# Splitting score chunks 9 to 7 and 10 to 6 between TensorE and VectorE at the layer ends of a two-layer decode kernel, with the last softmax moved ahead of V work

## Chip, cores, metric

One core of a Trainium2 chip. The metric is the device time of one execution in microseconds (us), lower is better. The runs of one kernel spread over 0.5 to 1.5 us here, and the differences of this case are of the same order, so medians and ranges are given.

## The reference, cut

Batch 2, one token, width 576, two identical layers. Each has an attention block over a given cache of 16384 keys and values (32 heads, head size 128, bfloat16) and an MLP block (576 to 4608 to 576).

```python
def _A_ref(x, k_cache, v_cache, wq, wo):
    q = (x @ wq).reshape(B, 1, 32, 128).transpose(0, 2, 1, 3)
    scores = jnp.einsum("bhqd,bhkd->bhqk", q, k_cache) * 128 ** -0.5
    p = softmax(scores)
    o = jnp.einsum("bhqk,bhkd->bhqd", p, v_cache)
    return o.transpose(0, 2, 1, 3).reshape(B, 1, 4096) @ wo
# _B_ref: layernorm, a shift term with w2, layernorm, gelu(. @ w3) @ w4, residuals
x = x + A(layernorm(x));  x = x + B(layernorm(x))     # layer 0
x = x + A(layernorm(x));  x = x + B(layernorm(x))     # layer 1, same weights and cache
```

The K and V loads are 126 x 8.39 MB = 1.06 GB for two layers, with almost no reuse: this is a stream from HBM.

## The kernel before

There are 64 *units* per layer (2 batches x 32 heads). A unit is one K and one V of 4 MiB. Its 128 blocks of 128 keys are cut into 16 *chunks* of 8. VectorE and TensorE share the score work:

- a chunk on TensorE is 8 transposes into PSUM, an eviction by ScalarE, and 8 one-column matmuls (the lines with `tps`, `ktsb`, `sps`);
- a chunk on VectorE (a *dot*) is one multiply by the broadcast query and one reduction (`prod`, `sd`).

V work (a *weighing*, `ops`) is 128 one-column matmuls. SBUF holds three *places*, each one K and one V; the weights reuse the same space, so loads wait until the tenant before is done. One queue (SyncE's) issues all loads in a fixed order. Layer 1 runs the units backwards, so the last two units of layer 0 stay in SBUF.

```python
W4_PIECES = (6, 3, 2, 1)          # w4 in 12 parts; the first piece shares w3's place
...
self.NCP = self.NCH // 2          # 8 of 16 chunks on TensorE, always
...
def weigh(self, l, i, h):
    vt, res = self.get("V", l, u, h)      # res: the loads of this half (two for the split last unit)
    def f(pe):
        for j in range(self.TB):
            ins = pe.matmul(self.ops[q][:, 0:1], lhsT=vt[:, j * 128:(j + 1) * 128], rhs=..., ...)
        return ins
    self.pe(f, r=[*res, f"p{q}"], w=[f"P:ops{q}"])
    self.release("V", l, u, h)
...
def attention(self, l):           # one unit per turn of the loop
    for i in range(U):
        early = l == 1 and 1 <= i <= 4
        dv = list(range(NCP, NCH))
        for c in range(NCP):
            self.turn(l, i, c)                       # transposes and eviction
            if len(self.waiting) > self.LEAD: self.score()
            if i >= 1 and c == 1: self.unit_max(l, i - 1)
            if i >= 1 and c == (3 if early else 4): self.exps(l, i - 1)
            if c >= 1:
                for _ in range(-(-len(dv) // (NCP - c))): self.dots(l, i, dv.pop(0))
            if i == U - 1 and c == 3:                # the "mid projection"
                self.weigh(l, i - 2, 0); self.weigh(l, i - 2, 1)
                self.normalize(*mid, ...); self.project_pieces(l, [self.n_wo - 1])
        now = i >= 1 and not early and i != U - 2
        if now: self.weigh(l, i - 1, 0)
        while self.waiting: self.score()
        if now: self.weigh(l, i - 1, 1)
        self.row_max(l, i)
        ...
    self.unit_max(l, U - 1); self.exps(l, U - 1); self.normalizers(...)
    self.normalize(other, ...)
    self.weigh(l, U - 1, 0); self.weigh(l, U - 1, 1)
    ...                                              # last projection, then the MLP
```

The mid projection matters for loads: the last quarter of the last V lies where wo's last piece lies, so it can't be loaded before. In layer 0 only one place is free for weights (the other two hold the kept units), so w4's later pieces wait until the first row blocks of w3 are used, and layer 1's wq waits for w3 and for w4's first piece.

Of the kernel before, what the change touches and what calls it, by code (L numbers as in the profile page):

```python
# [233 lines left out]
class Decode:  # L234
# [5 lines left out]
    ROT = 12  # L240
    WO_PIECE = 4
    FJ = 3
    W4_PIECES = (6, 3, 2, 1)

    def __init__(self, nc, A_x, K, V, wq, wo, w2, w3, w4, out):
        self.nc = nc
        self.A_x, self.K, self.V, self.wq, self.wo = A_x, K, V, wq, wo
        self.w2, self.w3, self.w4, self.out = w2, w3, w4, out
        self.B, Sq, self.D = A_x.shape
        _, self.H, self.S, self.Dh = K.shape  # L250
        self.F = w3.shape[1]
        assert Sq == 1 and self.Dh == 128 and self.B == 2
        self.KT = (self.D + 127) // 128
        self.klast = self.D - 128 * (self.KT - 1)
        self.p0 = 128 - self.klast
        assert self.p0 == 64
        self.MT = self.F // 128
        self.FA = self.MT // self.FJ
        assert sum(self.W4_PIECES) == self.FA
        self.U = self.B * self.H  # L260
        self.NB = self.S // 128
        self.TB = self.NB // 2
        self.NCH = self.NB // self.CH
        self.NCP = self.NCH // 2
        self.scale = float(self.Dh) ** -0.5
        n = self.H - 1 - self.N_MID
        self.n_wo = -(-n // self.WO_PIECE) + 1
        cuts = [*range(0, n, self.WO_PIECE), n, self.H - 1]
        self.wo_cuts = [cuts, [self.H - c for c in cuts]]
        self.s = Sched(nc)  # L270
        sb = nc.alloc_sbuf_tensor
        B, KT = self.B, self.KT
        self.half = self.TB * 128
        self.place_n = 4 * self.half
        self.buf = sb("buf", [128, 3 * self.place_n], BF16)
        self.ring = Arena(self.s, self.buf)
        self.ktsb = [sb(f"ktsb{i}", [128, self.CH, 128], BF16) for i in range(self.NKT)]
        self.prod = [sb(f"prod{i}", [128, self.CH, 128], BF16) for i in range(2)]
        self.ident = sb("ident", [128, 128], BF16)
        self.identS = sb("identS", [128, 128], FP32)  # L280
        self.qt = sb("qt", [128, self.U], BF16)
        self.qb = [sb(f"qb{i}", [128, 128], BF16) for i in range(2)]
        self.p = [sb(f"p{i}", [128, self.NB], BF16) for i in range(2)]
        self.sd = [sb(f"sd{i}", [128, self.TB], FP32) for i in range(2)]
        small = sb("small", [128, 11 + 4 * B], FP32)
        self.cinv, self.cone, self.ceps = small[:, 0:1], small[:, 1:2], small[:, 2:3]
        self.m1, self.m2, self.m, self.bias = (small[:, 3 + 2 * i:5 + 2 * i] for i in range(4))
        self.st = small[:, 11:11 + 2 * B].rearrange("p (a b) -> p a b", a=2)
        self.var, self.rstd = small[:, 11 + 2 * B:11 + 3 * B], small[:, 11 + 3 * B:11 + 4 * B]
        self.qcur = sb("qcur", [128, 2], BF16)  # L290
        self.wolast = sb("wolast", [128, self.D], BF16)
        self.lsum = sb("lsum", [128, self.U, 2], FP32)
        self.o = sb("o", [128, self.U], FP32)
        self.den = sb("den", [128, self.U], FP32)
        self.otn = sb("otn", [128, self.U], BF16)
        self.xa = sb("xa", [128, 2, KT, B], FP32)
        self.xb = sb("xb", [128, 2, KT, B], FP32)
        self.x1 = sb("x1", [128, 2, KT, B], FP32)
        self.hs = sb("hs", [128, KT, B], FP32)
        self.xc = sb("xc", [128, KT, B], FP32)  # L300
        self.xn = sb("xn", [128, KT, B], BF16)
        self.xnh = sb("xnh", [128, 2, B], BF16)
        self.sel = sb("sel", [128, 128], BF16)
        self.par = sb("par", [128, 2], FP32)
        self.xsum = sb("xsum", [128, KT, B], FP32)
        self.zero = sb("zero", [128, B], BF16)
        MB = self.MT * B
        flat = self.prod[0][:, :, :].rearrange("p a b -> p (a b)")
        self.zz, self.zu, self.ze, self.zr = (flat.bitcast(FP32)[:, i * MB:(i + 1) * MB] for i in range(4))
        self.gt = flat[:, 8 * MB:9 * MB]  # L310
        self.rows = flat[:, 0:self.D]
        ps = nc.alloc_psum_tensor
        self.tps = [ps(f"tps{i}", [128, self.CH * 128], BF16) for i in range(3)]
        self.sps = [ps(f"sps{i}", [128, 512], FP32) for i in range(2)]
        self.ops = [ps(f"ops{i}", [128, 512], FP32) for i in range(2)]
        self.misc = ps("misc", [128, 512], FP32)
# [348 lines left out]
    def query_rows(self, l, i):  # L665
# [4 lines left out]
        self.act(lambda a: a.activation(out=self.qb[q][:, :], in_=self.misc[:, 0:128], func=ACT.Copy),  # L670
                 r=["P:misc"], w=[f"qb{q}"])

    def turn(self, l, i, c):

        u = self.order[l][i]
        h, j0 = divmod(c * self.CH, self.TB)
        kt, res = self.get("K", l, u, h)
        b, k = c % 3, c % self.NKT

        def f(pe):  # L680
            for j in range(self.CH):
                ins = pe.transpose(self.tps[b][:, j * 128:(j + 1) * 128],  # L682
                                   kt[:, (j0 + j) * 128:(j0 + j + 1) * 128], self.ident[:, :])
            return ins
        self.pe(f, r=[*res, "ident"], w=[f"P:tps{b}"])
        self.act(lambda a: a.activation(out=self.ktsb[k][:, :, :].rearrange("p a b -> p (a b)"), in_=self.tps[b][:, :],  # L686
                                        func=ACT.Copy), r=[f"P:tps{b}"], w=[f"ktsb{k}"])
        self.waiting.append((l, i, c, k))
        if (c + 1) * self.CH == self.TB:
            self.release("K", l, u, 0)  # L690
# [13 lines left out]
    def dots(self, l, i, c):  # L704
        u = self.order[l][i]
# [4 lines left out]
        k3 = kt.rearrange("p (j d) -> p j d", d=128)[:, j0:j0 + self.CH, :]  # L710
        self.dve(lambda v: v.tensor_tensor(out=self.prod[d][:, :, :], in0=k3, in1=bcast_mid(self.qb[q][:, :], self.CH),  # L711
                                           op=ALU.mult), r=[*res, f"qb{q}"], w=[f"prod{d}"])
        o = c * self.CH - self.NCP * self.CH
        self.dve(lambda v: v.tensor_reduce(out=self.sd[q][:, o:o + self.CH], in_=self.prod[d][:, :, :], axis=AX.X,  # L714
                                           op=ALU.add), r=[f"prod{d}"], w=[f"sd{q}"])
        if (c + 1) * self.CH == self.NB:
            self.release("K", l, u, 1)

    def row_max(self, l, i):
        q = i % 2  # L720
        n = self.NCP * self.CH
        self.dve(lambda v: v.tensor_reduce(out=self.m1[:, q:q + 1], in_=self.sps[q][:, 0:n], axis=AX.X, op=ALU.max),  # L722
                 r=[f"P:sps{q}"], w=[f"m1{q}"])
        self.dve(lambda v: v.tensor_reduce(out=self.m2[:, q:q + 1], in_=self.sd[q][:, 0:self.NB - n], axis=AX.X,  # L724
# [12 lines left out]
    def exps(self, l, i):  # L737
        u = self.order[l][i]
        q = i % 2
        n = self.NCP * self.CH  # L740
        for part, (c0, c1, src, res) in enumerate(((0, n, self.sps[q][:, 0:n], f"P:sps{q}"),
                                                   (n, self.NB, self.sd[q][:, 0:self.NB - n], f"sd{q}"))):
            self.act(lambda a, c0=c0, c1=c1, src=src, part=part: a.activation(  # L743
# [4 lines left out]
    def weigh(self, l, i, h):  # L748
        u = self.order[l][i]
        q = i % 2  # L750
        vt, res = self.get("V", l, u, h)

        def f(pe):
            for j in range(self.TB):
                ins = pe.matmul(self.ops[q][:, 0:1], lhsT=vt[:, j * 128:(j + 1) * 128],  # L755
                                rhs=self.p[q][:, h * self.TB + j:h * self.TB + j + 1],
                                start=(h == 0 and j == 0), stop=(h == 1 and j == self.TB - 1))
            return ins
        self.pe(f, r=[*res, f"p{q}"], w=[f"P:ops{q}"])
        self.release("V", l, u, h)  # L760
        if h == 1 and i < self.U - 1:
            self.dve(lambda v: v.tensor_copy(out=self.o[:, u:u + 1], in_=self.ops[q][:, 0:1]),
                     r=[f"P:ops{q}"], w=["o"])
# [46 lines left out]
        self.project(parts[0][0], parts[-1][0] + parts[-1][1], parts)  # L810

    def attention(self, l):
        U, NCP, NCH = self.U, self.NCP, self.NCH
        self.waiting = []
        self.query(l, 0)
        self.query_rows(l, 0)
# [6 lines left out]
        for i in range(U):  # L823
# [1 line left out]
            if i == U // 2:  # L825
                self.load_wo_last(l)
            early = l == 1 and 1 <= i <= 4
            dv = list(range(NCP, NCH))
            for c in range(NCP):
                self.turn(l, i, c)  # L830
                if len(self.waiting) > self.LEAD:
                    self.score()
# [3 lines left out]
                    self.exps(l, i - 1)  # L836
                if i + 1 < U and c == 6:
                    self.query(l, i + 1)
                if c >= 1:
                    for _ in range(-(-len(dv) // (NCP - c))):  # L840
                        self.dots(l, i, dv.pop(0))
                if early and c == 5:
                    self.weigh(l, i - 1, 0)
                    self.weigh(l, i - 1, 1)
                if i == U - 1 and c == 3:
                    self.weigh(l, i - 2, 0)
                    self.weigh(l, i - 2, 1)
                    self.normalize(*mid, self.o[:, slice(*mid)], "o")
                    self.project_pieces(l, [self.n_wo - 1])
            now = i >= 1 and not early and i != U - 2  # L850
            if now:
                self.weigh(l, i - 1, 0)
            while self.waiting:
# [18 lines left out]
        self.exps(l, U - 1)  # L872
        self.normalizers(h * self.B, (h + 1) * self.B)
        other = self.order[l][-2]
        self.normalize(other, other + 1, self.o[:, other:other + 1], "o")
        self.weigh(l, U - 1, 0)
        self.weigh(l, U - 1, 1)
# [36 lines left out]
```

## Time and profile before

| | |
|---|---|
| time, median of 6 runs | 2578.36 us (2578.17 to 2578.93) |
| profiled span | 2576.7 us |
| moved | 1099.39 MB, 427 GB/s over the span |
| VectorE / TensorE busy | 77% / 60% |

The page of the profile of the kernel before: span, busy times, the rate in 40 slices of 64 us, and the totals of the DMA queues.

```profile
span 2576.7 us, 75357 instructions
...
PE 1546.0 (60%) x34519; PEld 1457.5 (57%) x34519; DVE 1978.0 (77%) x2781; ACT 1111.4 (43%) x1809; POOL 0.8 (0%) x10
...
GB/s 414 430 427 431 431 431 431 431 431 429 430 432 431 430 432 431 431 431 427 416 390 426 429 429 430 431 431 431 431 431 429 431 431 431 431 431 431 429 427 355
DMA packets 52927, 1099.39 MB, mean 427 GB/s; under 512 B 4996, under 2 KB 13256, under 8 KB 16968
```

The flat 431 is taken as the limit; only the first and last slices and the change of layers (416, 390, 426) are clearly lower. No engine is near its own limit on average (VectorE is the busiest, 77%). So the search is for short dips in the DMA rate. The table of time windows of the kernel before shows them; the columns are the window, its length, busy us (and count) of each engine, TensorE's granted clock, the DMA engines' busy share, and GB/s. A window counts a packet whole where it starts, so a short one can read above the limit.

```profile
core 0: us, PE busy (x) PEld busy (x) DVE busy (x) ACT busy (x) POOL busy (x), PEclk, DMA share, GB/s
1270.00:1272.00 2.00, 1.91 (x36) 1.91 (x37) 1.31 (x4) 0.43 (x1) 0.00 (x0) 0.50 0.77 287
...
1292.00:1294.00 2.00, 1.91 (x64) 1.88 (x65) 0.28 (x3) 0.00 (x0) 0.00 (x0) 0.50 0.93 382
1294.00:1296.00 2.00, 2.00 (x81) 2.00 (x79) 0.00 (x0) 0.00 (x0) 0.00 (x0) 0.50 0.70 212
1296.00:1298.00 2.00, 0.78 (x30) 0.69 (x27) 0.56 (x3) 0.49 (x2) 0.00 (x0) 0.50 0.93 342
1304.00:1306.00 2.00, 1.46 (x55) 1.37 (x53) 0.00 (x0) 0.00 (x0) 0.00 (x0) 0.50 0.73 273
...
1334.00:1336.00 2.00, 0.00 (x0) 0.00 (x0) 1.97 (x3) 0.00 (x0) 0.00 (x0) 0.50 0.64 266
1346.00:1348.00 2.00, 0.35 (x4) 0.35 (x4) 1.97 (x3) 0.00 (x0) 0.00 (x0) 0.50 0.99 279
...
1320.00:1360.00 40.00, 29.99 (x567) 28.83 (x565) 36.35 (x49) 23.66 (x36) 0.00 (x0) 0.58 0.98 401
```

The prediction calls these A (1268 to 1274), B (1292 to 1298), C (1304 to 1310), D (1320 to 1360) and, in layer 1, E (2534 to 2538).

At D the cause is VectorE. The order of time of SyncE's queue shows when the first loads of layer 1's steady part are issued, and VectorE's shows the start of each unit's row maximum, so the period of a unit:

```profile
1335.06 0.33 SPq L361 DMA_DIRECT2D buf<-in_A_k_cache_dram  x1
1345.27 0.33 SPq L361 DMA_DIRECT2D buf<-in_A_v_cache_dram  x1
1351.57 0.33 SPq L361 DMA_DIRECT2D buf<-in_A_k_cache_dram  x1
```

```profile
1336.20 0.21 DVE L722 TENSOR_REDUCE small<-sps 128x1 f32<-128x64 f32 x1
1352.71 0.21 DVE L722 TENSOR_REDUCE small<-sps 128x1 f32<-128x64 f32 x1
```

The period is 16.5 us: eight dots (0.68 + 1.22 us, overlapping a little, 1.85 us apart) and the maxima.

The end of layer 0, TensorE and VectorE in order of time: the two halves of unit 62's weighing, the row maximum of unit 63, then unit 63's weighing.

```profile
1274.78 1.84 PE L755 MATMUL ops<-p,buf 128*128 128x1 bf16 x64
1276.91 1.84 PE L755 MATMUL ops<-p,buf 128*128 128x1 bf16 x64
1278.87 0.21 DVE L722 TENSOR_REDUCE small<-sps 128x1 f32<-128x64 f32 x1
...
1281.86 3.55 PE L755 MATMUL ops<-p,buf 128*128 128x1 bf16 x128
```

### The profile page before, as it was taken

To read this page: it belongs to the slowest core of one execution; us is meant where nothing else is said; L and a number is where in the kernel's file an instruction comes from. 1 tells how busy PE (TensorE), PEld (TensorE's weight loads), DVE (VectorE), ACT (ScalarE), POOL (GpSimd) and SP (SyncE) were. 2 spreads that over 40 slices of the span, in tenths; PEclk is the share of its full clock that TensorE was granted. 3 is DMA by queue.
4 is the path that set the end of the run, shared out by engine and by line. 5 is a ranking of instruction groups with operands and counts; after the bars stand their busy time and mean duration, and the time that the engine had idled before them with its cause. 6 is when DMAs were issued, how large, how long until landed. Compare 5 with 4: busy or idle time off the path is not lost.

```text
span 2576.7 us, 75357 instructions
## 1 busy us (share of the span) xinstructions
PE 1546.0 (60%) x34519; PEld 1457.5 (57%) x34519; DVE 1978.0 (77%) x2781; ACT 1111.4 (43%) x1809; POOL 0.8 (0%) x10
## 2 busy tenths in 40 slices
PE   5656555656556555656667765556555565566666
PEld 4555555555455555556657765555555555555565
DVE  5877787778777777878759987777787787778875
ACT  3444444444344444444435544444444444444442
POOL 0000000000000000000000000000000000000000
PEclk8666666666666666666656666666666666666665
DMA  9999999999999999999999999999999999999998
GB/s 414 430 427 431 431 431 431 431 431 429 430 432 431 430 432 431 431 431 427 416 390 426 429 429 430 431 431 431 431 431 429 431 431 431 431 431 431 429 427 355
DMA packets 52927, 1099.39 MB, mean 427 GB/s; under 512 B 4996, under 2 KB 13256, under 8 KB 16968
## 3 DMA queue, kind: packets, MB, share of 16 engines
q1 hardware_dynamic: 52808, 1097.76, 99.6%
q8 instruction: 80, 1.31, 0.2%
q14 instruction: 39, 0.32, 0.0%
HBM read 1097.74 MB, written 0.00 MB: 426 GB/s over the span
## 4 chain that ended last, share of the span: by engine, by line
DMA 54%; DVE 38%; PE 6%; SPq 1%; issue 1%; ACT 0%; DVEq 0%
DMA buf<-in_A_k_cache_dram 52%; DVE sd L714 24%; DVE prod L711 13%; PE tps L682 4%; DMA buf<-in_B_w_dram 2%; PE misc L732 2%; SPq L392 1%; DVE small L734 1%; DMA buf<-in_A_wq_dram 0%; SPq L375 0%; PE misc L592 0%; DVE small L726 0%; DVE small L724 0%; DVE small L722 0%; PE misc L504 0%
## 5 line engine op out<-in xcount | busy, mean ns | idle before, releaser
L686 ACT ACTIVATE ktsb<-tps 128x1024 bf16<-128x1024 bf16 x1024 | 1004.7, 1029 | 886.7 <-PE tps L682 881.6
L714 DVE TENSOR_REDUCE sd<-prod 128x8 f32<-128x1024 bf16 x1024 | 1249.4, 1220 | 35.5
L682 PE MATMUL tps<-ident,buf 128*128 128x128 bf16 x8192 | 838.0, 269 | 644.6 <-DMA buf<-in_A_k_cache_dram 640.2
L682 PEld LDWEIGHTS tps<-ident,buf 128*128 128x128 bf16 x8192 | 680.4, 124 | 673.0 <-DMA buf<-in_A_k_cache_dram 660.3
L711 DVE TENSOR_TENSOR prod<-buf,qb 128x1024 bf16<-128x1024 bf16 x1024 | 697.9, 682 | 11.2 <-DMA buf<-in_A_k_cache_dram 10.3
L755 PE MATMUL ops<-p,buf 128*128 128x1 bf16 x16384 | 466.6, 165 | 180.7 <-DMA buf<-in_A_v_cache_dram 168.5
L755 PEld LDWEIGHTS ops<-p,buf 128*128 128x128 bf16 x16384 | 448.9, 102 | 191.4 <-DMA buf<-in_A_v_cache_dram 177.9
L699 PE MATMUL sps<-qcur,ktsb 128*128 128x1 bf16 x8192 | 352.4, 166 | 94.6 <-ACT ktsb L686 84.5
L734 DVE TENSOR_REDUCE small<-misc 128x1 f32<-128x128 f32 x128 | 37.3, 292 | 467.6 <-PE misc L732 467.6
L699 PEld LDWEIGHTS sps<-qcur,ktsb 128*128 128x128 bf16 x8192 | 316.5, 102 | 133.4 <-ACT ktsb L686 130.0
L670 ACT ACTIVATE qb<-misc 128x128 bf16<-128x128 f32 x128 | 35.5, 278 | 489.1 <-PE misc L667 489.1
L732 PE MATMUL misc<-identS,small 128*128 128x128 f32 x256 | 95.7, 477 | 48.1 <-DVE small L726 36.7
L732 PEld LDWEIGHTS misc<-identS,small 128*128 128x128 f32 x256 | 69.5, 332 | 52.3 <-DVE small L726 39.1
L743 ACT ACTIVATE p<-sd,small 128x64 bf16<-128x64 f32 x128 | 45.4, 354 | 0.0
L743 ACT ACTIVATE p<-sps,small 128x64 bf16<-128x64 f32 x128 | 40.7, 318 | 10.4 <-DVE small L734 10.4
L662 ACT ACTIVATE qcur<-qt 128x1 bf16<-128x1 bf16 x128 | 29.1, 227 | 19.4 <-DVE qt L599 19.4
L667 PE MATMUL misc<-ident,qcur 128*128 128x128 bf16 x128 | 34.1, 267 | 1.1 <-ACT qcur L662 1.1
L722 DVE TENSOR_REDUCE small<-sps 128x1 f32<-128x64 f32 x128 | 27.4, 214 | 0.0
L743 ACT ACTIVATION_READ_ACCUMULATOR p<-sps,small 128x1 f32 x128 | 27.1, 212 | 0.0
L724 DVE TENSOR_REDUCE small<-sd 128x1 f32<-128x64 f32 x128 | 26.7, 208 | 0.0
L743 ACT ACTIVATION_READ_ACCUMULATOR p<-sd,small 128x1 f32 x128 | 26.5, 207 | 0.0
L556 PE MATMUL sps<-xn,buf 128*128 128x2 bf16 x544 | 16.4, 165 | 14.0 <-DMA buf<-in_A_wq_dram 9.5
(75 smaller groups left out, 162.9 us busy)
## 6 DMA issues: line engine op xcount, KB each, us to landing
buf<-in_A_k_cache_dram SPq DMA_DIRECT2D x123, 4096.0 KB, 22.5
buf<-in_A_v_cache_dram SPq DMA_DIRECT2D x123, 4096.0 KB, 31.9
buf<-in_B_w_dram SPq DMA_DIRECT2D x8, 1152.0 KB, 18.3
buf<-in_A_wq_dram SPq DMA_DIRECT2D x8, 1024.0 KB, 8.6
buf<-in_A_wo_dram SPq DMA_DIRECT2D x14, 576.0 KB, 32.8
buf<-in_A_k_cache_dram SPq DMA_DIRECT2D x3, 2048.0 KB, 27.0
buf<-in_A_k_cache_dram SPq DMA_DIRECT2D x6, 1024.0 KB, 29.0
buf<-in_A_v_cache_dram SPq DMA_DIRECT2D x3, 2048.0 KB, 37.9
```

The costliest lines, as they stand in the source:

```text
L662: self.act(lambda a: a.activation(out=self.qcur[:, q:q + 1], in_=self.qt[:, u:u + 1], func=ACT.Copy), r=["qt"], w=[f"qcur{q}"])
L667: self.pe(lambda pe: pe.matmul(self.misc[:, 0:128], lhsT=bcast(self.qcur[:, q:q + 1], 128), rhs=self.ident[:, :], start=True, stop=True), ...
L670: self.act(lambda a: a.activation(out=self.qb[q][:, :], in_=self.misc[:, 0:128], func=ACT.Copy), r=["P:misc"], w=[f"qb{q}"])
L682: ins = pe.transpose(self.tps[b][:, j * 128:(j + 1) * 128], kt[:, (j0 + j) * 128:(j0 + j + 1) * 128], self.ident[:, :])
L686: self.act(lambda a: a.activation(out=self.ktsb[k][:, :, :].rearrange("p a b -> p (a b)"), in_=self.tps[b][:, :], func=ACT.Copy), r=[f"P:t ...
L699: ins = pe.matmul(self.sps[sp][:, col:col + 1], lhsT=self.ktsb[k][:, j, :], rhs=self.qcur[:, sp:sp + 1], start=True, stop=True)
L711: self.dve(lambda v: v.tensor_tensor(out=self.prod[d][:, :, :], in0=k3, in1=bcast_mid(self.qb[q][:, :], self.CH), op=ALU.mult), r=[*res, f ...
L714: self.dve(lambda v: v.tensor_reduce(out=self.sd[q][:, o:o + self.CH], in_=self.prod[d][:, :, :], axis=AX.X, op=ALU.add), r=[f"prod{d}"], ...
L732: self.pe(lambda pe: pe.matmul(self.misc[:, 128:256], lhsT=bcast(self.m[:, q:q + 1], 128), rhs=self.identS[:, :], start=True, stop=True), ...
L734: self.dve(lambda v: v.tensor_reduce(out=self.bias[:, q:q + 1], in_=self.misc[:, 128:256], axis=AX.X, op=ALU.max, negate=True), r=["P:misc ...
L743: self.act(lambda a, c0=c0, c1=c1, src=src, part=part: a.activation(out=self.p[q][:, c0:c1], in_=src, func=ACT.Exp, bias=self.bias[:, q:q ...
L755: ins = pe.matmul(self.ops[q][:, 0:1], lhsT=vt[:, j * 128:(j + 1) * 128], rhs=self.p[q][:, h * self.TB + j:h * self.TB + j + 1], start=(h ...
```

## The change

The intent: shift score work to TensorE where VectorE holds things up (9 of 16 chunks for the first twelve units of layer 1, 10 of 16 for the last three units of each layer); start the last unit's softmax earlier by putting unit U-2's weighing behind it; let the weighing wait for each piece of V by itself; and make w4's first piece smaller, so that the space it blocks is free sooner.

```diff
-    W4_PIECES = (6, 3, 2, 1)
+    W4_PIECES = (5, 4, 2, 1)
...
+    def ncp(self, l, i):
+        n = self.NCH // 2
+        if i >= self.U - 3:
+            return n + 2
+        return n + 1 if l == 1 and i < self.ROT else n
...                      (row_max, exps and dots take ncp(l, i) for NCP; the dots still start in the first 8 turns)
+        n = self.TB // len(res)
+        for k, part in enumerate(res):          # weigh: one wait for each load
+            def f(pe, k=k):
+                for j in range(k * n, (k + 1) * n): ...
+            self.pe(f, r=[part, f"p{q}"], w=[f"P:ops{q}"])
...
-                if i == U - 1 and c == 3:
+                if i == U - 1 and c == 7:
...
-            now = i >= 1 and not early and i != U - 2
+            self.release("K", l, self.order[l][i], 1)
+            now = i >= 1 and not early and i < U - 2
...                      (after the loop)
         self.exps(l, U - 1)
         self.normalizers(h * self.B, (h + 1) * self.B)
         other = self.order[l][-2]
+        self.weigh(l, U - 2, 0)
+        self.weigh(l, U - 2, 1)
         self.normalize(other, other + 1, self.o[:, other:other + 1], "o")
         self.weigh(l, U - 1, 0)
         self.weigh(l, U - 1, 1)
```

More of the change, by code (lines that the diff above doesn't have):

```diff
@@ L263, in __init__ @@
         self.NCH = self.NB // self.CH
-        self.NCP = self.NCH // 2
         self.scale = float(self.Dh) ** -0.5
@@ L712, in dots @@
                                            op=ALU.mult), r=[*res, f"qb{q}"], w=[f"prod{d}"])
-        o = c * self.CH - self.NCP * self.CH
+        o = (c - self.ncp(l, i)) * self.CH
         self.dve(lambda v: v.tensor_reduce(out=self.sd[q][:, o:o + self.CH], in_=self.prod[d][:, :, :], axis=AX.X,
                                            op=ALU.add), r=[f"prod{d}"], w=[f"sd{q}"])
-        if (c + 1) * self.CH == self.NB:
-            self.release("K", l, u, 1)
     def row_max(self, l, i):
         q = i % 2
-        n = self.NCP * self.CH
+        n = self.ncp(l, i) * self.CH
         self.dve(lambda v: v.tensor_reduce(out=self.m1[:, q:q + 1], in_=self.sps[q][:, 0:n], axis=AX.X, op=ALU.max),
@@ L739, in exps @@
         q = i % 2
-        n = self.NCP * self.CH
+        n = self.ncp(l, i) * self.CH
         for part, (c0, c1, src, res) in enumerate(((0, n, self.sps[q][:, 0:n], f"P:sps{q}"),
@@ L751, in weigh @@
         vt, res = self.get("V", l, u, h)
-        def f(pe):
-            for j in range(self.TB):
-                ins = pe.matmul(self.ops[q][:, 0:1], lhsT=vt[:, j * 128:(j + 1) * 128],
-                                rhs=self.p[q][:, h * self.TB + j:h * self.TB + j + 1],
-                                start=(h == 0 and j == 0), stop=(h == 1 and j == self.TB - 1))
-            return ins
-        self.pe(f, r=[*res, f"p{q}"], w=[f"P:ops{q}"])
+        n = self.TB // len(res)
+        for k, part in enumerate(res):
+            def f(pe, k=k):
+                for j in range(k * n, (k + 1) * n):
+                    ins = pe.matmul(self.ops[q][:, 0:1], lhsT=vt[:, j * 128:(j + 1) * 128],
+                                    rhs=self.p[q][:, h * self.TB + j:h * self.TB + j + 1],
+                                    start=(h == 0 and j == 0), stop=(h == 1 and j == self.TB - 1))
+                return ins
+            self.pe(f, r=[part, f"p{q}"], w=[f"P:ops{q}"])
         self.release("V", l, u, h)
@@ L812, in attention @@
     def attention(self, l):
-        U, NCP, NCH = self.U, self.NCP, self.NCH
+        U, NCH = self.U, self.NCH
         self.waiting = []
@@ L827, in attention @@
             early = l == 1 and 1 <= i <= 4
-            dv = list(range(NCP, NCH))
-            for c in range(NCP):
+            ncp = self.ncp(l, i)
+            dv = list(range(ncp, NCH))
+            for c in range(ncp):
                 self.turn(l, i, c)
@@ L838, in attention @@
                     self.query(l, i + 1)
-                if c >= 1:
-                    for _ in range(-(-len(dv) // (NCP - c))):
+                if 1 <= c < NCH // 2:
+                    for _ in range(-(-len(dv) // (NCH // 2 - c))):
                         self.dots(l, i, dv.pop(0))
```

## The prediction

> **What bounds the kernel now.** DMA. The page's totals give 1099.39 MB in a span of 2576.7 us, 427 GB/s. Steady stretches read 430 to 432 GB/s in the slices, where a unit (8.4 MB) takes 19.5 us, while VectorE needs about 16.5 us for one. [...] At 431 GB/s the bytes alone take about 2551 us, so all that any schedule can win is some 26 us, and about half of it is start, rate of the small weight rows, and the last tail. The rest are short holes, from the table of 2-us and 5-us windows (estimates: bytes missing against the neighbouring rate):
>
> - A, 1268 to 1274 us (344, 287, 389 GB/s): the queue processor waits until 1270.7 for the mid output projection, to load V's last quarter. About 1.2 us.
> - B, 1292 to 1298 (382, 212, 342): w4's second piece waits for w3's first products. About 1.5 us.
> - C, 1304 to 1310 (273, 379, 332): wq's second row block waits for w4's first piece. About 1.2 us.
> - D, 1320 to 1360, mean 401: layer 1 starts with VectorE-bound units of 16.5 us (eight dots of 0.68 + 1.22 us); K at 1335.06 and V at 1345.27 are issued late. About 2.5 us.
> - E, 2534 to 2538 (246, 332): as A, layer 1. About 1.3 us.
>
> **What the change does.** A chunk moved from VectorE to TensorE frees 1.85 us of VectorE and costs TensorE 1.4 us at clock 0.50 (1.01 + 0.40), about 1 us at full clock, and ScalarE 1.03 us.
>
> - D: a 9/7 unit takes about 14.7 us of VectorE. TensorE stood 4.9 us per unit before the maximum, so it stays just below VectorE. K comes about 1.9 us earlier, then V and the next K. Gain 1.5 to 2 us.
> - C: the smaller first w4 piece (5 of 12) ends about 1.4 us earlier. Gain 0.5 to 1 us. B loses part of it, since less is queued before the wait.
> - A and E: the 10/6 split removes TensorE's 6-us wait before unit 62's maximum (1255.2 to 1261.2), but adds four chunks, 5.7 us at half clock. The mid projection moves from the fourth chunk to the eighth, behind all six dots. I expect the last quarter of V issued 0 to 1.6 us later: 0 to 0.6 us lost each.
> - Last unit: softmax starts 2 to 3 us earlier, but two weighings (3.55 us each) now follow it instead of one. Its end stays near 1285.4, between 1 us earlier and 1.5 us later. V's last quarter lands at 1283.4, so little was there.
> - The end: w4's pieces are waited for (4.2, 0.5, 0.7 us), so DMA, not compute, ends the kernel; its last 8 us hardly move.
>
> [...]
>
> **Prediction.** 2575.5 us, 80% between 2571.5 and 2579.5. Faster by over 2%: 1%; within 2%: 98%; slower: 1%.
>
> **What would show it.** Right: 1320 to 1360 above 412 GB/s, K issued near 1333, units of 14.7 us there, the hole at 1304 smaller, V's last quarter not issued earlier. Wrong: units still 16.5 us (TensorE-bound), or holes A and E gone.
>
> **What would make it wrong.** TensorE staying at half clock and becoming the slower engine at layer ends; the weighings after the softmax ending later than I think, deepening B; or the holes being only fast DMA engines waiting for slow ones, so that filling them moves nothing.

D's gain of 1.5 to 2 us, C's of 0.5 to 1 less B's part, and A's and E's loss of up to 0.6 us each: the sum came to 2575.5 us, 2.9 us below the time before. Two figures, both from the trace of before. The records of TensorE's granted clock hold 0.50 and 1.00 alone; eight transposes and eight one-column matmuls take 1.01 + 0.40 us at 0.50 (from 614.72) and 0.61 + 0.34 us at 1.00 (from 616.69). And "rate of the small weight rows" is 410 GB/s from 2560 to 2565, with the DMA engines busy (share 1.02) and nearly all bytes in packets of 3456 bytes, against 430 GB/s from 500 to 600 with packets of 32768 bytes.

## The result, and the profile after

The median is 2576.78 us (2576.38 to 2576.99, 6 runs) against 2578.36 us: 1.6 us or 0.06% less. The ratio is 0.9993, with a 95% interval of 0.9981 to 1.0006. Ratios are computed as the mean time of one kernel's fast runs over that of the other's in the same rounds, so they are not quite the ratio of the medians. The two ranges do not overlap, and a second measurement (below, `after_again`) gives 2576.81 against 2578.37, so a gain of about 1.6 us is real but tiny. It lies inside the predicted range and 1.3 us from the predicted 2575.5; but that range (2571.5 to 2579.5) holds the time before as well, so the number alone proves little, and the parts of the prediction have to be checked one by one.

The page of the kernel after:

```profile
span 2574.8 us, 76099 instructions
...
PE 1556.6 (60%) x34903; PEld 1465.3 (57%) x34903; DVE 1935.1 (75%) x2733; ACT 1133.5 (44%) x1833; POOL 0.8 (0%) x10
...
GB/s 413 431 427 432 431 432 430 432 428 432 433 431 431 428 433 431 432 431 428 414 403 429 428 429 431 431 429 431 432 432 430 429 431 433 430 431 428 428 426 359
```

Slice 21, which holds layer 1's start, went from 390 to 403 GB/s. The windows of the kernel after, same columns:

```profile
1270.00:1272.00 2.00, 1.92 (x36) 1.93 (x37) 0.19 (x2) 0.45 (x1) 0.00 (x0) 0.50 0.74 279
...
1292.00:1294.00 2.00, 1.17 (x37) 1.14 (x38) 0.27 (x3) 0.47 (x2) 0.00 (x0) 0.50 0.70 288
1294.00:1296.00 2.00, 2.00 (x76) 2.00 (x76) 0.16 (x1) 0.00 (x0) 0.00 (x0) 0.50 0.28 113
1296.00:1298.00 2.00, 1.52 (x57) 1.43 (x54) 0.18 (x1) 0.23 (x1) 0.00 (x0) 0.50 0.83 207
1304.00:1306.00 2.00, 1.11 (x41) 1.12 (x42) 0.00 (x0) 0.00 (x0) 0.00 (x0) 0.50 1.06 443
...
1334.00:1336.00 2.00, 1.35 (x10) 1.28 (x11) 1.08 (x6) 0.00 (x0) 0.00 (x0) 0.50 1.22 492
1346.00:1348.00 2.00, 1.72 (x35) 1.63 (x32) 1.97 (x3) 1.69 (x2) 0.00 (x0) 0.50 1.04 426
...
1320.00:1360.00 40.00, 32.28 (x633) 30.58 (x634) 35.63 (x48) 25.52 (x38) 0.00 (x0) 0.63 1.01 424
```

A is unchanged, and E nearly so (274 and 352 GB/s from 2534 to 2538, against 246 and 332). B is much deeper. C is gone and D nearly. Adding up the bytes of the packets in the two traces, and calling the surplus over before a lead (in us at 431 GB/s), gives: level at 1290, 1.5 us behind at 1300, 0.2 behind at 1310, 0.1 behind at 1330, 1.9 ahead at 1360 and 2.5 ahead at 1450. So B cost 1.5 us of bytes, C returned 1.3, and D brought 2.0 by 1360 and 2.6 by 1450.

Layer 1's start in the kernel after, SyncE's queue and the row maxima:

```profile
1332.97 0.33 SPq L360 DMA_DIRECT2D buf<-in_A_k_cache_dram  x1
1343.13 0.33 SPq L360 DMA_DIRECT2D buf<-in_A_v_cache_dram  x1
1347.63 0.33 SPq L360 DMA_DIRECT2D buf<-in_A_k_cache_dram  x1
```

```profile
1334.06 0.22 DVE L726 TENSOR_REDUCE small<-sps 128x1 f32<-128x72 f32 x1
1348.82 0.23 DVE L726 TENSOR_REDUCE small<-sps 128x1 f32<-128x72 f32 x1
```

The period is 14.8 us, and all three loads are issued 2.1 to 3.9 us earlier.

The end of layer 0 in the kernel after: the row maximum of unit 63, then both weighings in one piece.

```profile
1274.11 0.24 DVE L726 TENSOR_REDUCE small<-sps 128x1 f32<-128x80 f32 x1 [3.27 <-PE sps L705]
...
1277.11 6.64 PE L761 MATMUL ops<-p,buf 128*128 128x1 bf16 x244
1285.69 0.46 PE L761 MATMUL ops<-p,buf 128*128 128x1 bf16 x12 [1.94 <-issue]
```

The softmax starts 4.8 us earlier than before, yet the last weighing ends at 1286.15 instead of 1285.41. The brackets name idle time ahead of a group and what ended it: TensorE stood still for 1.94 us, 12 matmuls from the end, and "issue" says that it waited for nothing that the profile shows. V's last quarter is not the reason: it was issued at 1270.67 and landed 12.2 us later, at 1282.9.

### The profile page after: what moved, and what is told of

It reads as the page before. It is cut to its first block, busy times and chain, and to the rows that moved or that the text cites. A ratio compares the mean times of both kernels' runs of the same rounds, so it can differ in the third digit from the quotient of the medians.

```text
span 2574.8 us, 76099 instructions
## 1 busy us (share of the span) xinstructions
PE 1556.6 (60%) x34903; PEld 1465.3 (57%) x34903; DVE 1935.1 (75%) x2733; ACT 1133.5 (44%) x1833; POOL 0.8 (0%) x10
## 4 chain that ended last, share of the span: by engine, by line
DMA 54%; DVE 35%; PE 8%; SPq 1%; ACT 1%; issue 1%; DVEq 0%
DMA buf<-in_A_k_cache_dram 52%; DVE sd L720 22%; DVE prod L717 12%; PE tps L688 5%; DMA buf<-in_B_w_dram 2%; PE misc L736 2%; ACT ktsb L692 1%; SPq L391 1%; DVE small L738 1%; DMA buf<-in_A_wq_dram 1%; PE ops L761 1%; SPq L374 0%; PE misc L591 0%; PE sps L705 0%; ACT p L747 0%
## 5 line engine op out<-in xcount | busy, mean ns | idle before, releaser
L692 ACT ACTIVATE ktsb<-tps 128x1024 bf16<-128x1024 bf16 x1048 | 1026.7, 1029 | 854.8 <-PE tps L688 849.8
L720 DVE TENSOR_REDUCE sd<-prod 128x8 f32<-128x1024 bf16 x1000 | 1220.1, 1220 | 34.6
L717 DVE TENSOR_TENSOR prod<-buf,qb 128x1024 bf16<-128x1024 bf16 x1000 | 681.5, 681 | 11.2 <-DMA buf<-in_A_k_cache_dram 10.3
L705 PE MATMUL sps<-qcur,ktsb 128*128 128x1 bf16 x8384 | 359.8, 166 | 102.5 <-ACT ktsb L692 91.5
L747 ACT ACTIVATE p<-sd,small 128x64 bf16<-128x64 f32 (+2 forms) x128 | 45.2, 353 | 0.0
L747 ACT ACTIVATE p<-sps,small 128x64 bf16<-128x64 f32 (+2 forms) x128 | 40.9, 319 | 4.5 <-DVE small L738 4.5
L726 DVE TENSOR_REDUCE small<-sps 128x1 f32<-128x64 f32 (+2 forms) x128 | 27.7, 216 | 6.6 <-PE sps L705 6.5
L728 DVE TENSOR_REDUCE small<-sd 128x1 f32<-128x64 f32 (+2 forms) x128 | 26.4, 206 | 0.0
L768 DVE COPY o<-ops 128x1 f32<-128x1 f32 x126 | 18.7, 149 | 9.5 <-PE ops L761 9.5
```

What stands on the lines that cost most here:

```text
L692: self.act(lambda a: a.activation(out=self.ktsb[k][:, :, :].rearrange("p a b -> p (a b)"), in_=self.tps[b][:, :], func=ACT.Copy), r=[f"P:t ...
L705: ins = pe.matmul(self.sps[sp][:, col:col + 1], lhsT=self.ktsb[k][:, j, :], rhs=self.qcur[:, sp:sp + 1], start=True, stop=True)
L717: self.dve(lambda v: v.tensor_tensor(out=self.prod[d][:, :, :], in0=k3, in1=bcast_mid(self.qb[q][:, :], self.CH), op=ALU.mult), r=[*res, f ...
L720: self.dve(lambda v: v.tensor_reduce(out=self.sd[q][:, o:o + self.CH], in_=self.prod[d][:, :, :], axis=AX.X, op=ALU.add), r=[f"prod{d}"], ...
L747: self.act(lambda a, c0=c0, c1=c1, src=src, part=part: a.activation(out=self.p[q][:, c0:c1], in_=src, func=ACT.Exp, bias=self.bias[:, q:q ...
```

## The experiments

Four questions: which part earned the 1.6 us; whether filling A, B and C is worth anything; whether the reordered softmax is; and what the pause is. All results were correct and all runs were fast ones, but for `dummy32`, which has a single run and so no known state. In each job the kernel before ran too, at 2578.18 to 2578.38 us. The kernel after did not run in the job (and on the chip) of `dummy32`, `hold_dot`, `pieces33` and `all3`, so these are set against its times from other chips; before agrees within 0.2 us between them.

### early_only: only the 9-to-7 split

```diff
 (kernel before)
+    def ncp(self, l, i):
+        n = self.NCH // 2
+        return n + 1 if l == 1 and i < self.ROT else n
```

> Kernel before with only the 9-to-7 split for layer 1's first twelve units. Theory (the gain is earned at the start of layer 1, where K and V are issued late): about 2.0 us off, 2576.2 to 2577.0, K of the fourth unit issued near 1333 instead of 1335.06, the dips at 1334 to 1352 gone, the dips at 1268, 1292 and 1304 unchanged. Rival (the gain comes from the layer ends): within 0.5 us of before, 2578.4.

Measured: 2578.23 us (2577.54 to 2579.07), before 2578.38. K was issued at 1333.33, and 1320 to 1360 ran at 412 GB/s instead of 401; the dips at 1334 and 1346 shrank (393 and 385 GB/s) but did not vanish. So the mechanism shows in the trace, but by itself 0.15 us came of it. The expectation of 2.0 us was missed; the rival's number (no change) was met, although for another reason than it gave.

### pieces_only: only the w4 pieces

```diff
 (kernel before)
-    W4_PIECES = (6, 3, 2, 1)
+    W4_PIECES = (5, 4, 2, 1)
```

> Kernel before with only the w4 pieces 5,4,2,1. Theory (a smaller first piece empties the queue earlier at 1292 and frees wq's second row block earlier at 1304, and the two cancel): total within 0.5 us of before; the dip at 1292 to 1298 deeper by about 1 us worth of bytes, the dip at 1304 to 1310 gone. Rival (the deeper dip at 1292 is only the later end of the last unit's V work): the dip at 1292 as before, and about 1 us off the total.

Measured: 2578.22 us (2577.84 to 2578.51). The windows at 1292, 1294 and 1296 read 268, 149 and 314 GB/s, deeper than before's 382, 212 and 342; the ones at 1304, 1306 and 1308 read 429, 411 and 442. The theory held: C was exchanged for B. A smaller first piece puts less into the queue ahead of the wait.

### ends_only: only the layer ends

```diff
 (kernel after)
-    W4_PIECES = (5, 4, 2, 1)
+    W4_PIECES = (6, 3, 2, 1)
-        return n + 1 if l == 1 and i < self.ROT else n
+        return n
```

> Kernel after without the 9-to-7 split in layer 1 and with w4 pieces 6,3,2,1: only 10-to-6 at the layer ends, the reordered softmax and the waits by V piece. Theory: no gain, 2578.0 to 2579.0; the last V work in layer 0 ends at about 1286 instead of 1285.4, with a pause of about 1.9 us inside it. Rival (the layer ends gain): 2577.0 or less.

Measured: 2578.95 us (2578.18 to 2579.39), so no gain, as expected. In layer 0 the last V work ended at 1286.26 with a pause of 1.92 us in it, as expected too; in layer 1 it ended at 2551.44 against before's 2551.18, with a pause of 1.95 us in it.

### order_back: unit U-2's V work ahead of the softmax again

```diff
 (kernel after)
-            now = i >= 1 and not early and i < U - 2
+            now = i >= 1 and not early and i != U - 2
...
-        self.weigh(l, U - 2, 0)
-        self.weigh(l, U - 2, 1)
```

> Kernel after with the last-but-one unit's V work put back ahead of the last softmax. Theory (two weighings back to back, 512 TensorE instructions, outrun its instruction supply): the pause of 1.9 us inside the last weighing is gone or much shorter, but the softmax starts about 3.5 us later; the last V work ends within 1 us of after's 1286.15, total within 0.5 us of after. Rival (the pause belongs to V's late landing or to a fixed place in the program): the pause stays inside the last weighing and the V work ends later than 1287.

Measured: 2576.92 us (2576.54 to 2577.01), the same as after. TensorE in order of time, layer 0, in this kernel:

```profile
1275.16 1.63 PE L761 MATMUL ops<-p,buf 128*128 128x1 bf16 x56
1278.80 0.35 PE L761 MATMUL ops<-p,buf 128*128 128x1 bf16 x8 [2.01 <-issue]
1282.24 3.55 PE L761 MATMUL ops<-p,buf 128*128 128x1 bf16 x128
```

The total and the end of V work (1285.79) came as the theory said, and the last weighing is free of the pause; but the pause had only moved into the weighing of unit 62. (The row maximum came at 1279.26, 5.2 us later than in after, not 3.5.) So the reordering is worth nothing either way here, and "two weighings back to back" is too narrow a cause. From the pause to the end of V work it is now 8 + 2 + 2 + 128 = 140 matmuls, against 12 in after: exactly 128 more.

### dummy32: 32 idle matmuls ahead of the last weighings

```diff
 (kernel after)
         self.exps(l, U - 1)
+        def idle(pe):
+            for j in range(32):
+                ins = pe.matmul(self.misc[:, 500:501], lhsT=self.ident[:, :], rhs=self.ident[:, 0:1],
+                                start=True, stop=True)
+            return ins
+        self.pe(idle, r=["ident"], w=["P:misc"])
         self.normalizers(h * self.B, (h + 1) * self.B)
```

> Kernel after with 32 more TensorE matmuls (into an unused column) while TensorE waits for the last exponentials. Theory (the pause in the last weighing is the instruction supply, tied to the place in the instruction stream): in layer 0 it moves from 244 matmuls into the two weighings to about 212, in layer 1 from 221 to about 189, still 1 to 2 us long. Rival (tied to V's data or to the place inside the weighing): it stays at 244 and 221.

Measured: 2577.61 us in one run. The weighings in order of time in this kernel, layer 0 and layer 1:

```profile
1277.27 5.79 PE L761 MATMUL ops<-p,buf 128*128 128x1 bf16 x212
1284.66 1.31 PE L761 MATMUL ops<-p,buf 128*128 128x1 bf16 x44 [1.60 <-issue]
...
2541.75 4.33 PE L761 MATMUL ops<-p,buf 128*128 128x1 bf16 x157
2548.08 2.78 PE L761 MATMUL ops<-p,buf 128*128 128x1 bf16 x99 [2.00 <-issue]
```

And in layer 1 of the kernel after:

```profile
2540.91 6.03 PE L761 MATMUL ops<-p,buf 128*128 128x1 bf16 x221
2548.68 1.07 PE L761 MATMUL ops<-p,buf 128*128 128x1 bf16 x35 [1.73 <-issue]
```

In layer 0 the pause moved from 244 to 212, exactly 32 matmuls earlier, although V's last quarter landed as before (1283.05). In layer 1 it moved from 221 to 157, that is 64 earlier. The expectation of 189 forgot that layer 0's 32 extra matmuls lie ahead of layer 1 in the same stream; 32 + 32 is 64. The pause is tied to a place in TensorE's instruction stream. What lies at that place shows in the DMA queues: beside the loads, the trace has packets of 16384 bytes on a queue of their own, which it labels "instruction". The view of DMA queues of the kernel after, from 1283.0 to 1283.1, has one:

```profile
q8 instruction: 1, 0.02, 63.6%
```

It ran from 1283.07 to 1284.09, and TensorE went on at 1285.69. Over all 14 traces, 236 pauses of TensorE above 0.15 us are put down to "issue", and every one of them ends 1.2 to 1.6 us after the end of such a packet. In the long middle of layer 0, where TensorE's program is a loop (`Fori`), no trace has such a packet or such a pause (91 to 1130 us). So the pauses go with these packets. That TensorE waits there for the instructions which a packet brings is the author's reading; the trace names neither the engine nor the instructions that a packet is for. Most of the packets come without a pause: before has 80 of them and 13 pauses, after 83 and 20. In `hold_dot` (next) TensorE waits 1.46 us for V while the packet of 1281.59 is under way, and at the old place, after 244 matmuls, only 0.22 us of pause are left.

### hold_dot: the mid projection no longer behind six dots

```diff
 (kernel after)
-                if 1 <= c < NCH // 2:
+                if i == U - 1:
+                    if 1 <= c <= 5 or c == 8:
+                        self.dots(l, i, dv.pop(0))
+                elif 1 <= c < NCH // 2:
```

> Kernel after with the last of the six dots of the last unit held back until the mid projection is issued (chunk 8). Theory (the dips at 1270 and 2534 come from the mid projection standing behind six dots on VectorE): V's last quarter issued about 1.8 us earlier (near 1268.9 instead of 1270.67), both dips shallower by 0.5 to 0.8 us each, the last V work ending about 1.5 us earlier: total 2575.0 to 2576.0. Rival (those dips are fast DMA engines waiting for slow ones and cost nothing at the end): total as after, 2576.8 within 0.4.

Measured: 2577.5 us (2577.01 to 2578.07), slower than after by 0.7 us if anything. SyncE's queue and TensorE in order of time in this kernel:

```profile
1269.04 0.33 SPq L357 DMA_DIRECT2D buf<-in_A_v_cache_dram  x1
...
1320.62 0.43 SPq L354 DMA_DIRECT2D buf<-in_A_v_cache_dram  x1
```

```profile
1275.47 6.19 PE L761 MATMUL ops<-p,buf 128*128 128x1 bf16 x224
1283.12 0.69 PE L761 MATMUL ops<-p,buf 128*128 128x1 bf16 x20 [1.46 <-DMA buf<-in_A_v_cache_dram]
1284.03 0.46 PE L761 MATMUL ops<-p,buf 128*128 128x1 bf16 x12 [0.22 <-issue]
```

V's last quarter was issued 1.6 us earlier, but it landed at 1283.08, no earlier than after's 1282.91. The last weighing ended at 1284.5 instead of 1286.15, and by 1300 the bytes were 1.4 us ahead of after's. Yet the first V load of layer 1, which waits until wq has been used, was issued at 1320.62, against 1320.29 in the kernel after and 1320.58 before. The early lead is worth nothing: w4's last piece landed at 1308.16 (after: 1307.99, before: 1308.21) and the last of wq at 1319.51 (1319.19, 1319.48). The rival's reading held, though 2577.5 lies 0.3 us above its range too.

### pieces33: w4 in pieces 3, 3, 3, 2, 1

```diff
 (kernel after)
-    W4_PIECES = (5, 4, 2, 1)
+    W4_PIECES = (3, 3, 3, 2, 1)
-                if c == 1:
+                if c == 2:
```

> Kernel after with w4 in pieces 3,3,3,2,1, the first two in place 1 (so six parts are queued before the wait, as in before, and the region of wq's second row block is freed after three parts). Theory: the dip at 1292 to 1298 is back to before's depth (212 GB/s in its worst 2 us instead of 113), the dip at 1304 stays away; about 1 us of bytes gained by 1320; total 2575.6 to 2576.6. Rival (the dip at 1292 is set by the late end of the V work alone): the dip stays as in after.

Measured: 2577.22 us (2576.89 to 2577.46). The windows from 1292 read 390, 214 and 274 GB/s, and from 1304 414, 426 and 418: B was back to before's depth and C stayed away, as the theory said, and by 1320 the bytes were 0.9 us ahead of after's. By 1360 that lead was gone, and the total is not better: the theory's 2575.6 to 2576.6 was missed. A trace that looks better at the place worked on, and no gain.

### all3: held dot, pieces 3,3,3,2,1, and the normalizer matmul after unit U-2's V work

The edits of the last two kernels, and:

```diff
-        self.normalizers(h * self.B, (h + 1) * self.B)
         other = self.order[l][-2]
         self.weigh(l, U - 2, 0)
         self.weigh(l, U - 2, 1)
+        self.normalizers(h * self.B, (h + 1) * self.B)
```

> Kernel after with the held dot, pieces 3,3,3,2,1, and the last-but-one unit's V work issued before the normalizer matmul instead of after it. Theory: the gains add, 2574.0 to 2575.5. Rival (TensorE pauses and engine skew eat them): 2576 or more.

Measured: 2577.5 us (2577.11 to 2577.72). The bytes were 2.5 us ahead of after's at 1310; V's last quarter, issued 2 us earlier than in after, landed at 1282.94, and the first V load of layer 1 was issued at 1320.33, both as in after. The gains did not add, as the rival said. None of these three kernels beats the change itself.

### no_early, no_pieces, no_ends, after_again: the change with one part left out

`no_early` is the kernel after with the second line of `ncp`'s return set to `n`; `no_pieces` is after with `W4_PIECES = (6, 3, 2, 1)`; `no_ends` is `early_only` with `W4_PIECES = (5, 4, 2, 1)`; `after_again` is the kernel after, unedited.

> Kernel after without the 9-to-7 split in layer 1 (the layer ends and the w4 pieces stay). Additive theory (from early_only -0.15, pieces_only -0.16, ends_only +0.57 against before): 2578.6, and at most 0.3 us between it and before. Rival (the parts need each other: the earlier K and V at layer 1's start are what carries after): also about 2578.4, but then no_pieces and no_ends fall below 2577.5.

> Kernel after with w4 pieces 6,3,2,1. Additive theory: 2578.6. Rival (early split and layer ends together carry the gain; the pieces are a mere exchange of one dip for another): 2577.0 within 0.4.

> Kernel before with the 9-to-7 split in layer 1 and the w4 pieces 5,4,2,1, layer ends as before. Additive theory: 2577.9. Rival (TensorE pauses of about 2 us, whose places shift with every edit of the program, decide between the variants more than the parts do): anything from 2576.5 to 2578.5, with the difference seen in the last 40 us as a pause in the w3 or w4 products or in the V work.

> Kernel after itself on this chip, to join the runs of several jobs: 2576.8 within 0.3 if chip and time do not matter; before at 2578.3.

With these all eight combinations of the three parts are measured (medians, us):

| | layer ends as before | layer ends changed |
|---|---|---|
| neither | 2578.37 (before) | 2578.95 (ends_only) |
| 9-to-7 | 2578.23 (early_only) | 2577.17 (no_pieces) |
| pieces | 2578.22 (pieces_only) | 2577.97 (no_early) |
| 9-to-7 and pieces | 2577.50 (no_ends) | 2576.81 (after_again) |

The additive theory fell: it expected 2578.6 for `no_early` and `no_pieces`, 2577.9 for `no_ends`, and the sum of single effects for the whole, which would be slower than before. The average of the four kernels with a part less the average of the four without is -0.95 us for the 9-to-7 split, -0.55 for the pieces and -0.35 for the layer ends. Single medians wander by a few tenths (one kernel's runs spread by 0.5 to 1.5 us), so the order is better supported than the sizes. Of the rivals, `no_pieces` came within its 2577.0 plus or minus 0.4; `no_early`, at 2577.97, came between its rival's 2578.4 and after; the range of `no_ends`'s rival was too wide to test anything.

Part of the misfit has a place. In the profiles of before, `pieces_only`, `no_pieces` and after, the output is written 27.4 us after V's last quarter of layer 1 landed. In `early_only`, `ends_only`, `no_early` and `no_ends` it is 28.3 to 28.5 us: one of the w3 loads lands 0.9 us late there. These are the four kernels with just one of the 9-to-7 split and the layer ends. All four also have a pause of 1.66 to 1.92 us in the last w3 products, but so has `dummy32` (1.94 us), which takes 27.4 us, so the pause is not what costs. With this step taken off (an estimate, from one profile for each kernel), the single effects are -1.1 us for the 9-to-7 split, -0.2 for the pieces and -0.3 for the ends, and their sum is the gain measured, although `no_ends` and `no_early` then come out about 0.7 and 1.0 us faster than the sums of theirs. Why the load lands late is open.

## Why the prediction was right, point by point

- **DMA bounds the kernel, a gain of a few us at most.** Right: 2576.78 was measured, 2575.5 predicted.
- **D, "Gain 1.5 to 2 us".** The mechanism was right in every sign that was named: K at 1332.97, units of 14.8 us where TensorE did not hold them up (one of the next was 15.7), 424 GB/s. The bytes gained in the window are 40 us x (424 - 401) GB/s, or 2.1 us at 431 GB/s. The size did not carry over to the end: over the eight combinations about 1 us of it was left in the total, and alone almost nothing.
- **C gains, "B loses part of it".** C's sign was right. B lost all of it: 1.5 us of bytes against 1.3. `pieces_only` shows that the smaller piece does this by itself.
- **A and E, "0 to 1.6 us later".** V's last quarter was issued at the same time in layer 0 (1270.67 in both) and 0.9 us earlier in layer 1. More important, the value that the prediction gave these dips was wrong: `hold_dot`, `pieces33` and `all3` filled A, B or both in part and gained nothing.
- **Last unit, "between 1 us earlier and 1.5 us later".** 0.7 us later, for a reason that was not in the sum: a pause of 1.94 us in the instruction stream ate the lead of a softmax that was 4.8 us earlier, not "2 to 3 us". Part of that size is TensorE's clock: 1260 to 1270 ran at a mean of 0.77 instead of 0.50. The prediction named a faster clock as a possibility, but did not count it. What sets the clock is not shown: it stayed at 0.50 from 1270 to 1280 in before, with TensorE busy for 9.21 of the 10 us, and in after through 6.64 us of weighing without a gap.
- **The end, "its last 8 us hardly move".** Right: V's last quarter of layer 1 landed at 2545.84 instead of 2547.76, and the output was written at 2573.23 instead of 2575.13, both 1.9 us earlier. So nothing was won after that landing.

So the size of the total is partly luck: B took back what C gave, and A and E, which the prediction took for a loss of up to 0.6 us each, brought nothing when they were filled.

"The holes being only fast DMA engines waiting for slow ones" was one of the things that the prediction said would make it wrong. That filling them moves nothing is what the runs show for A, B and C: with these dips filled in whole or in part, layer 1's first loads landed no more than 0.3 us earlier than in before. The trace of before shows loads by size and the median time from issue to landing, here the three V loads issued from 1238.74 to 1239.58:

```profile
buf<-in_A_v_cache_dram SPq DMA_DIRECT2D x1, 4096.0 KB, 34.5
buf<-in_A_v_cache_dram SPq DMA_DIRECT2D x1, 2048.0 KB, 39.1
buf<-in_A_v_cache_dram SPq DMA_DIRECT2D x1, 1024.0 KB, 41.1
```

They landed at about 1273, 1278 and 1281. So in dip A (busy share 0.77 at 1270) three loads were still under way: the queue was not empty, but not all engines were busy. The packets of the trace say the same: with the queue full, about 16 are under way at a time; from 1269.5 to 1271.5 it is nine to thirteen, never fewer. For each load the trace also holds 16 updates of its semaphore, and the landing is the last of them. In before, those of the V load issued at 1238.74 come from 1262.29 to 1273.26, 11.0 us apart. For V's last quarter, issued in dip A, they are 8.3 us apart (1274.85 to 1283.12), for w4's last piece, issued in B, 5.4 us (1302.77 to 1308.21), and for the last of wq, issued in C, 3.8 us (1315.64 to 1319.48). So the parts of a load land far apart, and over A, B and C they drew together by 7.2 us. That these parts are the work of separate engines is the author's reading. A load that comes earlier into a dip brings more bytes at that moment, but what is waited for is its last part: in `hold_dot` V's last quarter was issued 1.6 us earlier, and by 1300 the bytes were 1.4 us ahead, but it landed no earlier (1283.08 against 1282.91). A spread of this kind shows at the very end of before, when no further load follows: 12 or fewer packets are under way from 2565.1 on and two or fewer from 2570.1 on, but the last one ends at 2572.45. The window of 2570.5 to 2572.5 (busy share 0.09 of 16 engines, so one or two):

```profile
2570.50:2572.50 2.00, 1.29 (x48) 1.21 (x46) 0.00 (x0) 0.00 (x0) 0.00 (x0) 0.50 0.09 36
```

That what is late in the dips is also what is late at the end is not shown, since the trace does not name the engines. Shown is that in all 14 traces layer 1's first new K and V were issued within 0.9 us of each other (1307.8 to 1308.6, 1320.1 to 1321.0), whatever the bytes did before.

**What stays open:** why after's lead over before, 2.0 us in landings at 1460, is 0.9 to 1.0 us from 2173 to 2527 and 1.9 us again at the last V (in bytes it falls from 2.5 us at 1450 to 1.4 at 2400), and why one w3 load lands late in four of the kernels.

## What to carry to other kernels

In this DMA-bound kernel dips in the rate, in which loads were still under way (three at 1270, at a busy share of 0.77), were not worth filling; so look for loads that are still under way in the dip, and check whether landings and the next gate (the next load that waits for data) move, not whether the curve looks smoother. When the remaining gain is a few tenths of a per cent, measure all combinations of a change's parts: one-at-a-time tests said that none of the three parts gains, and together they gain 1.6 us; in their profiles two of these tests lost 0.9 us in the last w3 loads, which only the trace tells. And in unrolled code that issues TensorE instructions as fast as these weighings do (128 matmuls and 128 weight loads in 3.55 us), look for pauses at fixed places of the instruction stream: here they took up to about 2 us in the weighings shown and moved by exactly the number of matmuls put in ahead (32 and 64), and the part of layer 0 in a loop (91 to 1130 us) had none.
